# A softmax-attention backward kernel: part of every fourth K load moved to the first seven DMA engines

## The chip, the core and the metric

The kernel runs on one core of a Trainium2 chip. That core has a matrix engine (TensorE, "PE" in the profile, with its weight loads as "PEld"), a vector engine (DVE), a scalar engine (ACT), GpSimd (POOL) and SyncE (SP), which here only issues transfers, and it has 16 DMA engines that move data between the chip's memory (HBM) and the on-chip memory (SBUF). The metric is the device time of one execution in microseconds. Lower is better.

## The reference

One query row per head attends to 8192 keys; the forward output and the gradients of q, k and v are returned, all in bfloat16.

```python
B, H, Sq, Skv, Dh = 1, 32, 1, 8192, 128      # q, grad_out: (1,32,1,128)  k, v: (1,32,8192,128)

def _fwd_reference(q, k, v):
    scale = q.shape[-1] ** -0.5
    scores = jnp.einsum('bhqd,bhkd->bhqk', q, k) * scale
    attn = _softmax(scores, axis=-1)
    return jnp.einsum('bhqk,bhkd->bhqd', attn, v)

def reference(q, k, v, grad_out):
    _out, _vjp = jax.vjp(_f, q, k, v)         # _f is _fwd_reference
    _grads = _vjp(grad_out)
    return (_out, *_grads)                    # out, dq, dk, dv
```

For each head K and V (2 MB each) are read, and dk and dv (2 MB each) are written: 8 MB per head and 268 MB in all. dk and dv are outer products, so they are as large as K and V, and almost all of the traffic is in these four tensors.

## The kernel before

Each head's K is one tile of 128 partitions by 64 slots of 128 values: partition p holds the 64 consecutive rows 64p to 64p+63, which are 16 KB without a gap in HBM. A load of a whole K is one transfer of 128 rows of 16384 bytes. The pools hold three K tiles and two V tiles.

```python
CH = 16
K_BUFS = 3
V_BUFS = 2
NST = 2
# P = 128 partitions, NT = 64 slots, NCH = 4, H = 32 heads

    def rows_of(x, h, c, parts):
        L = NT // parts
        return x[0, h].rearrange("(p n) d -> p n d", p=P)[:, c * L:(c + 1) * L, :]

    def load_k(h):
        Kt[h] = kpool.tile([P, NT, D], BF16, tag="K", name="Kt")
        parts = NCH if h == 0 else 1
        for c in range(parts):
            nc.sync.dma_start(slots(Kt[h], c, parts), rows_of(k, h, c, parts))

    def load_v(h):
        Vt[h] = vpool.tile([P, NT, D], BF16, tag="V", name="Vt")
        parts = NCH if h in (0, H - 1) else 1
        for c in range(parts):
            nc.sync.dma_start(slots(Vt[h], c, parts), rows_of(v, h, c, parts))
    # ... (cut)
    def outer(h, which, r):
        # ... one quarter of dk or dv on DVE, then, for every half (a quarter in the last head):
        parts = 4 if h == H - 1 else NST
        if r % (4 // parts) == 4 // parts - 1:
            c = r // (4 // parts)
            nc.sync.dma_start(rows_of(dst, h, c, parts), slots(G, c, parts))
```

The main loop, cut to what issues transfers and what they serve; p_ is the head before:

```python
    for h in range(H + 1):
        p_ = h - 1
        if h < H:
            for u in range(NCH):
                k_blocks(h, u)              # DVE transposes K in blocks
            k_scores(h)                     # PE: scores
            if 0 < h < H - 1:
                load_v(h + 1)
        if h > 0:
            ds_of(p_); outer(p_, "dk", 0); dq_of(p_, 0)
        # ... (softmax of head h, partly)
        if h > 0:
            dq_of(p_, 1); outer(p_, "dk", 1)        # stores the first half of dk
        if 0 < h and h + 2 < H:
            load_k(h + 2)
        # ... (maximum, exp, sum)
        if h > 0:
            outer(p_, "dk", 2); outer(p_, "dk", 3)  # stores the second half of dk
        # ... (V transposes on PE, output, dP)
        outer(h, "dv", 0); outer(h, "dv", 1); outer(h, "dv", 2); outer(h, "dv", 3)  # two stores of dv
```

All these transfers are issued by SyncE on one queue. So a head has six of them: V, half of dk, K, half of dk, and two halves of dv.

Of the kernel before, what the change touches and what calls it, by code (L numbers as in the profile page):

```python
# [18 lines left out]
V_BUFS = 2  # L19
NST = 2  # L20
QD = 32


@with_exitstack
def kernel(
# [11 lines left out]
    nc = tc.nc  # L37
    P = 128
    _, H, S, D = k.shape
    assert D == P and S % (P * CH) == 0 and H <= P  # L40
    NT = S // P
    NCH = NT // CH
    NQ = P // QD
    assert NCH == 4 and NQ == 4
    W = D // 2
    NB = W // QD
    scale = float(D) ** -0.5
# [13 lines left out]
    Kt, Vt, XK, XV, st = {}, {}, {}, {}, {}  # L61
# [5 lines that stand above are left out]
    def slots(X, c, parts):  # L67
        L = NT // parts
        return X[:, c * L:(c + 1) * L, :]

    def load_k(h):
        Kt[h] = kpool.tile([P, NT, D], BF16, tag="K", name="Kt")
        parts = NCH if h == 0 else 1
        for c in range(parts):
            nc.sync.dma_start(slots(Kt[h], c, parts), rows_of(k, h, c, parts))

    def load_v(h):
        Vt[h] = vpool.tile([P, NT, D], BF16, tag="V", name="Vt")
        parts = NCH if h in (0, H - 1) else 1
        for c in range(parts):  # L80
            nc.sync.dma_start(slots(Vt[h], c, parts), rows_of(v, h, c, parts))

    rows = consts.tile([H, 2, D], BF16)
    nc.sync.dma_start(rows[:, 0, :], q.rearrange("b h s d -> (b h s) d"))
    nc.sync.dma_start(rows[:, 1, :], grad_out.rearrange("b h s d -> (b h s) d"))
    load_k(0)
    load_v(0)
    load_k(1)
    load_v(1)

    ident = consts.tile([P, P], BF16)
# [6 lines left out]
    nc.vector.reduce_sum(in_quad[:], ident[:].rearrange("p (a i) -> p a i", a=NQ), axis=AX.X)  # L98
    lane = consts.tile([P, QD], F32)
    nc.vector.reduce_sum(lane[:], ident[:].rearrange("p (a i) -> p i a", a=NQ), axis=AX.X)  # L100
# [3 lines left out]
    for w in range(NB):  # L104
        for e2 in range(2):
            four = consts.tile([H, NQ, QD], BF16, tag=f"four{w}{e2}")
            nc.vector.tensor_copy(
                four[:], rows[:, 0, :].rearrange("h (w j e) -> h w e j", w=NB, e=2)[:, w, e2:e2 + 1, :]
                .to_broadcast([H, NQ, QD]))
            tp = psT.tile([P, CH, P], BF16, tag="T")  # L110
# [17 lines left out]
    def k_blocks(h, u):  # L128


        if u == 0:
            XK[h] = ktpool.tile([P, CH, NB, NCH, QD], F32, tag="XK", name="XK_sb")
        nc.vector.transpose(XK[h][:, :, :, u, :],  # L133
# [94 lines left out]
# [3 lines that stand above are left out]
            x = st[h] = {}  # L231
            for u in range(NCH):
                k_blocks(h, u)
            k_scores(h)
            if 0 < h < H - 1:
                load_v(h + 1)
# [10 lines left out]
        if 0 < h and h + 2 < H:  # L247
            load_k(h + 2)
# [88 lines left out]
```

## Time and profile before

| | |
|---|---|
| time, median of three | 667.74 us (667.62 to 667.99) |
| span of the profiled execution | 667.0 us |
| PE busy | 516.8 us (77%) |
| DVE busy | 512.5 us (77%) |
| ACT busy | 182.1 us (27%) |
| bytes moved | 269.94 MB, mean 405 GB/s |
| HBM read, written | 134.23 MB each |

How to read it: the profile records each instruction of every engine and each packet of the DMA engines. "Busy" is the time in which an engine ran an instruction. The rows of 40 digits or numbers cut the span into 40 equal slices; a DMA digit of 9 means that in this slice the 16 DMA engines were busy for 90% or more on average. A DMA queue's share is the time its packets took on all 16 engines. A wait names who waited, at which line, for whom, and then the total in us, the number of waits and the longest. In the list of issues the last column is the median time from the issue of a transfer to its landing, which includes the time it stood behind earlier ones. [...]

### The profile page before, as it was taken

To read this page: it belongs to the slowest core of one execution; us is meant where nothing else is said; L and a number is where in the kernel's file an instruction comes from. 1 tells how busy PE (TensorE), PEld (TensorE's weight loads), DVE (VectorE), ACT (ScalarE), POOL (GpSimd) and SP (SyncE) were. 2 spreads that over 40 slices of the span, in tenths; PEclk is the share of its full clock that TensorE was granted. 3 is DMA by queue.
4 is the path that set the end of the run, shared out by engine and by line. 5 is a ranking of instruction groups with operands and counts; after the bars stand their busy time and mean duration, and the time that the engine had idled before them with its cause. 6 is when DMAs were issued, how large, how long until landed. Compare 5 with 4: busy or idle time off the path is not lost.

```text
span 667.0 us, 23105 instructions
## 1 busy us (share of the span) xinstructions
PE 516.8 (77%) x10727; PEld 485.8 (73%) x10727; DVE 512.5 (77%) x658; ACT 182.1 (27%) x321; POOL 0.7 (0%) x6
## 2 busy tenths in 40 slices
PE   2887988888887777878779787787776888778881
PEld 1887878878877767877668676677766777677870
DVE  4797888888877797777877778777788776887762
ACT  0333323232323222232222322223312223223230
POOL 0000000000000000000000000000000000000000
PEclk9995556566565565555555655666557665555555
DMA  8999999999999999999999999999999999999783
GB/s 330 414 425 424 419 427 414 424 423 426 425 425 424 425 425 424 425 429 423 423 427 426 423 416 422 413 412 418 395 423 418 397 416 406 409 420 403 270 357 142
DMA packets 29807, 269.94 MB, mean 405 GB/s; under 512 B 3472, under 2 KB 3472, under 8 KB 6032
## 3 DMA queue, kind: packets, MB, share of 16 engines
q1 hardware_dynamic: 29712, 268.48, 97.0%
q8 instruction: 83, 1.36, 0.7%
q14 instruction: 12, 0.10, 0.0%
HBM read 134.23 MB, written 134.23 MB: 403 GB/s over the span
## 4 chain that ended last, share of the span: by engine, by line
DMA 75%; PE 17%; DVE 3%; ACT 2%; issue 1%; SPq 0%; ACTq 0%
DMA Kt<-in_k_dram 26%; DMA Vt<-in_v_dram 26%; DMA out_dram<-G_dv 23%; PE T_ps L168 7%; PE s_ps L145 2%; PE dp_ps L185 2%; PE m_ps L185 2%; PE dp_ps L180 1%; DVE XK_sb L133 1%; ACT XT_sb L170 1%; PE m_ps L255 1%; DVE G_dk L195 1%; PE m_ps L268 1%; PE s_ps L161 0%; ACT qd L211 0%
## 5 line engine op out<-in xcount | busy, mean ns | idle before, releaser
L168 PE MATMUL T_ps<-ident,Vt 128*128 128x128 bf16 x2048 | 228.7, 302 | 31.9 <-DMA Vt<-in_v_dram 31.9
L168 PEld LDWEIGHTS <-Vt 128*128 128x128 bf16 x2048 | 201.1, 142 | 33.8 <-DMA Vt<-in_v_dram 33.6
L133 DVE STREAM_TRANSPOSE XK_sb<-Kt 128x1024 f32<-128x1024 f32 x128 | 148.2, 1213 | 81.1 <-DMA Kt<-in_k_dram 81.1
L170 ACT COPY XT_sb<-T_ps 128x1024 f32<-128x1024 f32 x128 | 129.5, 1012 | 189.7 <-PE T_ps L168 189.7
L195 DVE TENSOR_TENSOR G_dk<-ds_rep,qd 128x2048 bf16<-128x2048 bf16 x128 | 155.7, 1219 | 1.1
L195 DVE TENSOR_TENSOR G_dv<-p_rep,qd 128x2048 bf16<-128x2048 bf16 x128 | 148.2, 1220 | 8.5 <-ACT p_rep L277 8.5
L180 PEld LDWEIGHTS <-XT_sb 128*128 128x128 bf16 x2048 | 74.7, 106 | 27.2 <-ACT XT_sb L170 27.2
L180 PE MATMUL dp_ps<-doT,XT_sb 128*128 128x1 bf16 x2048 | 73.6, 166 | 24.4 <-ACT XT_sb L170 24.4
L145 PE MATMUL s_ps<-q_blk,XK_sb 128*128 128x4 bf16 x2048 | 59.1, 168 | 23.2 <-DVE pdt L216 20.5
L145 PEld LDWEIGHTS <-XK_sb 128*128 128x128 bf16 x2048 | 56.5, 103 | 25.5 <-DVE pdt L216 22.3
L185 PE MATMUL dp_ps<-ds_rep,Kt 128*128 128x1 bf16 x2048 | 64.7, 165 | 6.6 <-issue 6.0
L185 PEld LDWEIGHTS <-Kt 128*128 128x128 bf16 x2048 | 59.9, 104 | 12.3 <-issue 12.3
L185 PEld LDWEIGHTS <-Vt 128*128 128x128 bf16 x2048 | 61.1, 105 | 0.0
L185 PE MATMUL m_ps<-p_rep,Vt 128*128 128x1 bf16 x2048 | 60.5, 166 | 0.0
L226 ACT COPY dq_all<-dp_ps 128x1 f32<-128x1 f32 x32 | 5.1, 159 | 173.9 <-PE dp_ps L185 173.9
L268 PEld LDWEIGHTS m_ps<-rs,ones_f 128*128 128x128 f32 x64 | 16.0, 310 | 48.6 <-ACT e L267 48.6
L268 PE MATMUL m_ps<-rs,ones_f 128*128 128x1 f32 x64 | 18.7, 360 | 39.2 <-ACT e L267 39.2
L264 DVE TENSOR_REDUCE nbias<-m_ps 128x1 f32<-128x128 f32 x32 | 9.3, 292 | 22.0 <-ACT qd L211 22.0
L255 PE MATMUL m_ps<-diag,ones_f 128*128 128x128 f32 x64 | 25.3, 499 | 0.7 <-DVE diag L253 0.7
L218 DVE SCALAR_TENSOR_TENSOR ds_rep<-dp_ps,pdt,p_s 128x256 bf16<-128x256 f32 x32 | 15.5, 484 | 12.0 <-PE dp_ps L180 9.6
L277 ACT ACTIVATE p_rep<-e,rinv 128x256 bf16<-128x256 f32 x32 | 16.2, 507 | 30.3 <-DVE rinv L275 30.3
L211 ACT CAST qd<-m_ps 128x256 bf16<-128x256 f32 x32 | 11.9, 372 | 42.4 <-PE m_ps L207 42.4
(40 smaller groups left out, 163.0 us busy)
## 6 DMA issues: line engine op xcount, KB each, us to landing
Kt<-in_k_dram SPq DMA_DIRECT2D x31, 2048.0 KB, 28.0
out_dram<-G_dv SPq DMA_DIRECT2D x62, 1024.0 KB, 25.8
out_dram<-G_dk SPq DMA_DIRECT2D x62, 1024.0 KB, 28.0
Vt<-in_v_dram SPq DMA_DIRECT2D x30, 2048.0 KB, 28.3
Vt<-in_v_dram SPq DMA_DIRECT2D x8, 512.0 KB, 13.8
Kt<-in_k_dram SPq DMA_DIRECT2D x4, 512.0 KB, 5.4
out_dram<-G_dv SPq DMA_DIRECT2D x4, 512.0 KB, 16.9
out_dram<-G_dk SPq DMA_DIRECT2D x4, 512.0 KB, 10.7
```

Source lines behind the costliest of these rows:

```text
L133: nc.vector.transpose(XK[h][:, :, :, u, :], slots(Kt[h], u, NCH).rearrange("p g d -> p (g d)").bitcast(F32).rearrange("p (g w j) -> p g w ...
L145: nc.tensor.matmul(out[:, g, :], lhsT=cols[:, g, c // 2, c % 2], rhs=q_blk[:, h, c, :], start=(c == 0), stop=(c == 2 * NB - 1), skip_group ...
L168: nc.tensor.transpose(T_ps[:, i, :], Vt[h][:, c * CH + i, :], ident[:])
L170: nc.scalar.copy(X.rearrange("p c s -> p (c s)").bitcast(F32), T_ps.rearrange("p c s -> p (c s)").bitcast(F32))
L180: nc.tensor.matmul(st[h]["dp"][:, n:n + 1], lhsT=X[:, i, :], rhs=doT[:, h:h + 1], start=True, stop=True, skip_group_check=True)
L185: nc.tensor.matmul(out_col, lhsT=Xt[:, n, :], rhs=rep[:, n, 0:1], start=(n == 0), stop=(n == NT - 1), skip_group_check=True)
L195: nc.vector.tensor_tensor(slots(G, r, 4).rearrange("p n (a b) -> p n a b", b=R), slots(rep, r, 4).unsqueeze(2).to_broadcast([P, Q, D // R, ...
L211: nc.scalar.copy(x["qd"][:].rearrange("p a d -> p (a d)"), x["m"][:, 256:512])
L218: nc.vector.scalar_tensor_tensor(out=x["ds"][:], in0=x["dp"][:, 0:NT].unsqueeze(2).to_broadcast([P, NT, R]), scalar=pdt[:], in1=x["p_s"][: ...
L255: nc.tensor.matmul(x["m"][:, 128:256], lhsT=ones_f[:], rhs=diag[:], start=True, stop=True, skip_group_check=True)
L268: nc.tensor.matmul(x["m"][:, 0:1], lhsT=ones_f[:], rhs=rs[:], start=True, stop=True, skip_group_check=True)
L277: nc.scalar.activation(x["p"][:], e[:].unsqueeze(2).to_broadcast([P, NT, R]), ACT.Copy, scale=rinv[:])
```

## The change

Every fourth K load (heads 2, 6, 10, ..., 30) is no longer one transfer of 128 rows of 64 slots. It becomes three: all 128 partitions with slots 0 to 43, the first 119 partitions with slots 44 to 63, and the last 9 partitions with slots 44 to 63. The 119-row part is meant to run on the first seven DMA engines alone, so that these carry more of the traffic and the other nine less. Also, the V load of the last head is cut into halves instead of quarters. The bytes moved and all arithmetic are as before.

```diff
+LIGHT_EVERY = 4
+LIGHT_SLOTS = 20

     def load_k(h):
         Kt[h] = kpool.tile([P, NT, D], BF16, tag="K", name="Kt")
-        parts = NCH if h == 0 else 1
-        for c in range(parts):
-            nc.sync.dma_start(slots(Kt[h], c, parts), rows_of(k, h, c, parts))
+        if h == 0:
+            for c in range(NCH):
+                nc.sync.dma_start(slots(Kt[h], c, NCH), rows_of(k, h, c, NCH))
+        elif h % LIGHT_EVERY != LIGHT_EVERY // 2:
+            nc.sync.dma_start(Kt[h][:], rows_of(k, h, 0, 1))
+        else:
+            src = rows_of(k, h, 0, 1)
+            m = NT - LIGHT_SLOTS
+            for rng, cut in ((slice(0, P), slice(0, m)), (slice(0, 119), slice(m, NT)),
+                             (slice(119, P), slice(m, NT))):
+                nc.sync.dma_start(Kt[h][rng, cut, :], src[rng, cut, :])

     def load_v(h):
         Vt[h] = vpool.tile([P, NT, D], BF16, tag="V", name="Vt")
-        parts = NCH if h in (0, H - 1) else 1
+        parts = NCH if h == 0 else 2 if h == H - 1 else 1
```

## The prediction, made before the changed kernel was run

> **What bounds the kernel now.** I read the page from the DMA rows down: which resource is never idle, then who waits for whom, then how the 16 DMA engines differ. First the page's slices, queues and chain:
>
> ```profile
> DMA  8999999999999999999999999999999999999783
> GB/s 330 414 425 424 419 427 414 424 423 426 425 425 424 425 425 424 425 429 423 423 427 426 423 416 422 413 412 418 395 423 418 397 416 406 409 420 403 270 357 142
> q1 hardware_dynamic: 29712, 268.48, 97.0%
> q8 instruction: 83, 1.36, 0.7%
> ...
> DMA 75%; PE 17%; DVE 3%; ACT 2%; issue 1%; SPq 0%; ACTq 0%
> ```
>
> The queue keeps the 16 engines busy for 97% of the span, while PE and DVE stand at 77%; the chain is 75% DMA. So bytes per engine set the time, and the bytes are not changed. What can change is their share per engine. The stretches of the span show when a share is lost (columns: busy us of PE, PEld, DVE, ACT, POOL, then clock, DMA share, GB/s):
>
> ```profile
> 280.00:360.00 80.00, 64.70 (x1296) 60.92 (x1294) 61.02 (x77) 21.59 (x39) 0.00 (x0) 0.50 1.01 425
> ...
> 480.00:560.00 80.00, 60.52 (x1302) 56.57 (x1300) 63.27 (x80) 21.43 (x38) 0.00 (x0) 0.61 1.00 411
> ...
> 610.00:640.00 30.00, 24.28 (x510) 22.50 (x508) 24.26 (x34) 7.25 (x16) 0.00 (x0) 0.50 0.83 320
> 640.00:667.00 27.00, 11.00 (x236) 10.51 (x233) 9.37 (x14) 4.21 (x6) 0.00 (x0) 0.56 0.55 218
> ```
>
> 425 GB/s falls to 411 in the second half, and the last 57 us run at 320 and 218: some engines wait for others. The DMA queue's own waits say why:
>
> ```profile
> SPq L203 <- DMA out_dram<-G_dk: 111.7, 52, 2.5
> SPq L203 <- DMA Kt<-in_k_dram: 110.8, 26, 5.2
> SPq L75 <- DMA Vt<-in_v_dram: 97.5, 23, 4.5
> ```
>
> The issuing queue waits for earlier DMAs. In the trace the transfers use eight semaphores in turn, and from 400 to 610 us 60 of 61 issues come within 0.15 us of the last landing of the transfer eight places before; from 40 to 150 us only 1 of 36 does. So no engine can be more than eight transfers ahead of the slowest.
>
> Which engine is slow? The trace holds the 16 landing counts of every transfer. [...] For V loads issued at 83.15 and 383.48 us (15 heads apart) I get (us, landing):
>
> ```
> issued    first     8th    15th    last
>  83.15    97.8     99.1   101.9   101.9
> 383.48   391.2    399.7   402.1   411.8
> 590.66   598.2    600.6   606.5   619.0
> ```
>
> First engine: (391.15-97.79)/15 = 19.56 us per head. Last: (411.80-101.92)/15 = 20.66, and (618.98-411.80)/10 = 20.72 afterwards. ONE engine loses 1.1 us per head, is last in every transfer, and never rests until 666 us. Following the others, lags at 385 us are: seven engines at 0, 0.1, 0.2, 0.2, 0.3, 1.1 and 3.3; eight at 7.3 to 9.4; the slow one at 19.1. The eight are pushed back in turn by about 1.5 us at a time, with the instruction queue's fetches (q8, one packet of 0.9 to 1.1 us some 8 us apart). The slow one's store packets take up to 380 ns where the rest need 309; its load packets are as the others'.
>
> [...]
>
> I choose the reading that the slow one is engine 7, the seven fast ones are 0 to 6 and the eight that fetches hit are 8 to 15. The count 7 + 1 + 8 fits, and a split onto exactly the first seven fits it too. It is an inference.
>
> **The change, part by part.** Light heads are h = 2, 6, ..., 30: 8 loads of 31. Busy engines start a 16384 B packet every 0.607 us (611 ns less 4 overlap), an 8192 B one every 0.3055, a 4096 B one every 0.1553, by the packet records. The line through the outer two gives estimates of 0.419 us for 11264 B (44 slots) and 0.193 for 5120 B (20 slots); a completion packet takes 0.006.
>
> 1. K load before, per engine: 8*0.607+0.006 = 4.86 us.
> 2. Light load, engines 0-6: 8*0.419+0.006 + 17*0.193+0.006 + 0.193+0.006 = 6.84 us: +1.98.
> 3. Engines 7 and 8: 8*0.419+0.006+0.193+0.006 = 3.56 us: -1.31.
> 4. Engines 9-15: 3.36 us: -1.50.
> 5. Over 8 loads: engine 7 saves 10.5 us, and this all lies on the path, since that engine is busy from 3 to 666 us. Engines 0-6 gain 15.8 us of work, beside it.
> 6. Does another engine take over? Per head the slow one goes from 20.68 to 20.68-1.31/4 = 20.35. Engines 0-6: 19.56+1.98/4 = 20.06; the worst of them (its lag grew from 1.0 to 3.3 us in 15 heads, so 19.71) gets 20.21. Engines 8-15 lose 84/8 fetches of 1.5 us in 32 heads, 0.49 a head: 19.56+0.49-1.31/4 = 19.72 at most. It just holds.
> 7. Sixteen more issues: the queue issues some 0.5 us apart at the start (1.64, 2.10, 2.57), while transfers wait 5 to 25 us in the engines' rings. Hidden. But with eight semaphores in turn, a head of 8 transfers instead of 6 lets the queue reach one head ahead (8 MB, some 20 us) instead of 1.3. The slow engine still holds 15 us of work at each issue. Hidden.
> 8. Last V load in halves: four packets of 4096 B become two of 8192, 32*0.155-16*0.306 = 0.08 us less per engine, and two semaphores come free where the queue stalls near 626 us. Compute may start one quarter (1.3 us) later, but the tail has room: the last dk stores are issued at 651.4 to 655.8 and the slow engine reaches them only at 660.8.
>
> The tail: by the chain in order of time, compute goes from the landing of the last K (626.5) to the last store's data at 655.4. Both shift by the slow engine's gain, and the store backlog still ends later than compute. Sum: 667.74-10.5-0.1 = 657.1 us; a little for new collisions: 657.3, a gain of 1.6%.
>
> The issue table gives the sizes I used:
>
> ```profile
> Kt<-in_k_dram SPq DMA_DIRECT2D x31, 2048.0 KB, 28.0
> out_dram<-G_dv SPq DMA_DIRECT2D x62, 1024.0 KB, 25.8
> ...
> Vt<-in_v_dram SPq DMA_DIRECT2D x30, 2048.0 KB, 28.3
> Vt<-in_v_dram SPq DMA_DIRECT2D x8, 512.0 KB, 13.8
> ```
>
> **Rivals.**
> A. *The slow engine is among 9 to 15* (say 15) while 0 to 6 are free of fetches: it saves 8*1.50 = 12.0 us, 655.6. Against: eight engines are fetch-hit, and if those were the upper eight the slow one would lie in the lower eight.
> B. *The fetch-hit eight are engines 0 to 7.* Then 0-6 go to 19.56+0.49+0.50 = 20.55 per head against the old 20.68: a new bound takes the place of the old, at most 32*0.13 = 4 us are won, and the time stays at 663 to 667.
> C. *The slow engine is one of 0 to 6.* It gets 15.8 us more: 683.5. For: nothing in the trace numbers engines. Against: the seven fastest just fill that set.
> D. *Compute or the semaphores become the bound.* DVE waits 81.1 us for K in 24 waits and PE 31.9 us for V, so compute has slack of about 2.5 us a head (81.1/32) against a gain of 0.33; but the shorter reach of the queue in light heads could eat 1 to 4 us: 658 to 661.
>
> **Range and chances.** Main reading about 0.8, A 0.06, B 0.07, C 0.05. Within the main reading I expect 655.5 to 661. Faster by 2% means below 654.4, beyond even A; I give 0.08. Slower by 2% needs C (0.07). Range 654.6 to 663.
>
> **What would show it.** Right: the last landing runs behind the first by clearly less than 21 us from 400 us on (about 0.3 us growth per head instead of 1.1); K transfers of 1408, 595 and 45 KB; the slices stay near 425 GB/s to 600 us; the last-V landing moves from 639.7 to about 629; the final two slices hold higher rates. Wrong: seven engines last in each light load (B), or a lag that grows faster (C), or DMA share under 9 in the middle (D). The weakest link is the engine number.

## The result, and the profile after

The changed kernel takes 699.39 us (median of 4 runs, 698.27 to 700.65) against 667.68 us before: a ratio of 1.0477, 95% interval 1.0455 to 1.0499. That is 31.7 us slower, where 657.3 was predicted and 683.5 was the worst rival.

The slices, queue and chain of the changed kernel, in the form shown of before (40 equal slices of a span of 698.8 us):

```profile
DMA  8999999999999998999989999899998999979963
GB/s 334 396 424 424 425 425 357 421 424 427 402 329 422 424 425 356 339 425 423 425 349 344 427 425 422 339 359 426 428 424 315 379 426 426 426 286 389 418 277 137
...
q1 hardware_dynamic: 30576, 268.48, 94.2%
...
DMA 78%; PE 13%; DVE 5%; ACT 1%; issue 1%; SPq 0%; ACTq 0%; DVEq 0%
```

The same bytes now leave the 16 engines idle for 6% of the span instead of 3%. Between dips the rate is the old 425 GB/s; the dips recur at the pace of the light loads, one in four heads. The stretches of the span show it closely (columns as before: from:to, length, busy us of the five compute engines, clock, DMA share, GB/s). The first two are the stretches shown of before, the last two are one light load and the time after it:

```profile
280.00:360.00 80.00, 58.54 (x1200) 55.34 (x1199) 57.33 (x71) 21.67 (x36) 0.00 (x0) 0.55 0.97 393
480.00:560.00 80.00, 62.80 (x1325) 58.91 (x1323) 58.32 (x75) 22.04 (x39) 0.00 (x0) 0.59 0.96 391
...
270.00:295.00 25.00, 18.47 (x376) 17.33 (x373) 18.12 (x23) 6.67 (x11) 0.00 (x0) 0.50 0.90 332
300.00:345.00 45.00, 32.23 (x678) 29.68 (x675) 33.44 (x44) 11.91 (x23) 0.00 (x0) 0.58 1.01 426
```

393 and 391 GB/s stand against 425 and 411 before. The issue table of the changed kernel has the three parts as planned:

```profile
Kt<-in_k_dram SPq DMA_DIRECT2D x8, 1408.0 KB
Kt<-in_k_dram SPq DMA_DIRECT2D x8, 595.0 KB
...
Kt<-in_k_dram SPq DMA_DIRECT2D x8, 45.0 KB
```

The waits of the issuing queue, in the changed kernel, are still waits for earlier transfers:

```profile
SPq L215 <- DMA out_dram<-G_dk: 102.9, 50, 2.4
SPq L215 <- DMA Kt<-in_k_dram: 89.9, 20, 5.5
...
SPq L79 <- DMA Vt<-in_v_dram: 53.6, 12, 5.1
```

So DMA remains the bound, and the question is which engine is last. The completion counts of one light load answer it. In the trace of the kernel before, each of the 209 transfers, of 32 or 128 rows, has 16 of these counts on its semaphore, and there are as many packets of 4 B as counts, 3344. A count is read here as the landing of one engine's share, and its distance to the first count of the transfer as that engine's lag; no trace says which engine a count is from. The lags keep: from one 128-row transfer to the next, the counts put in order of time move against the first by 0.03 us in the median, and nine in ten by under 0.37. In the changed kernel the 128-row part has 16 counts, the 119-row part 7 and the 9-row part 9 (us; from the trace's semaphore times, without one further count that each of the two smaller parts has 0.4 to 0.7 us after its issue):

```
44 slots, 128 rows, issued 89.49:  102.4 102.5 103.2 103.9 104.0 104.0 104.1 105.3 105.9
                                   106.5 106.9 107.2 107.7 111.6 111.7 112.8
20 slots, 119 rows, issued 89.88:  111.8 112.0 112.9 113.7 117.3 117.7 118.7
20 slots,   9 rows, issued 92.35:  102.9 103.0 112.1 112.4 113.1 114.3 117.5 117.9 119.0
dk half,  128 rows, issued 94.85:  105.0 to 108.4 (nine), 114.4 to 121.2 (seven)
```

The part that was to go to fast engines ends at 118.7 and 119.0, and the last engine of the next transfer, 121.2, is one of the seven. This suggests that the slow engine is among those that were given more. Also, by the prediction's estimate the 119-row part should take 17*0.193 = 3.3 us per engine; matched in order, the seven take 5.2 to 6.0.

### The profile page after: what moved, and what is told of

Read it like the earlier page. It is cut to its first block, busy times and chain, and to the rows that moved or that the text cites. A ratio compares the mean times of both kernels' runs of the same rounds, so it can differ in the third digit from the quotient of the medians.

```text
span 698.8 us, 23136 instructions
## 1 busy us (share of the span) xinstructions
PE 521.1 (75%) x10727; PEld 489.5 (70%) x10727; DVE 513.9 (74%) x658; ACT 182.1 (26%) x321; POOL 0.7 (0%) x6
## 4 chain that ended last, share of the span: by engine, by line
DMA 78%; PE 13%; DVE 5%; ACT 1%; issue 1%; SPq 0%; ACTq 0%; DVEq 0%
DMA Kt<-in_k_dram 39%; DMA Vt<-in_v_dram 16%; DMA out_dram<-G_dv 15%; DMA out_dram<-G_dk 8%; PE T_ps L180 5%; DVE XK_sb L145 2%; PE s_ps L157 2%; PE m_ps L197 1%; PE dp_ps L197 1%; DVE G_dk L207 1%; PE dp_ps L192 1%; ACT XT_sb L182 1%; PE m_ps L267 1%; PE m_ps L280 0%; PE s_ps L173 0%
## 5 line engine op out<-in xcount | busy, mean ns | idle before, releaser
L180 PE MATMUL T_ps<-ident,Vt 128*128 128x128 bf16 x2048 | 231.9, 305 | 49.2 <-DMA Vt<-in_v_dram 49.0
L197 PEld LDWEIGHTS <-Kt 128*128 128x128 bf16 x2048 | 59.9, 104 | 11.7 <-issue 11.7
```

The costliest lines, as they stand in the source:

```text
L180: nc.tensor.transpose(T_ps[:, i, :], Vt[h][:, c * CH + i, :], ident[:])
L197: nc.tensor.matmul(out_col, lhsT=Xt[:, n, :], rhs=rep[:, n, 0:1], start=(n == 0), stop=(n == NT - 1), skip_group_check=True)
```

## The experiments

Theory 1: the slow engine is one of 0 to 6 (rival C), so the change gave it more bytes. Theory 2: the packets of parts that cover only some of the 128 partitions are themselves slow. Rivals: short packets, more transfers, or the row spacing in HBM. In every table of steps below, a step is the time from one transfer's last landing to the next one's last landing, all parts of a K taken as one. The engine landing last is taken to be engine 4 in all of these runs, except in the run with 12 slots on engines 0 to 3, which is not in the table. The engines were numbered in one run; the runs stood on several chips, so elsewhere the number 4 is an inference unless the run itself shows it.

**The last V in halves alone.**

```diff
-        parts = NCH if h in (0, H - 1) else 1
+        parts = NCH if h == 0 else 2 if h == H - 1 else 1
```

> The kernel before with the last V load in halves, K loads as before. Both theories put the loss into the light K loads, so the time stays at 667.7 within 1 us. If it is over 672, the tail is part of the loss.

Measured: 667.89 us against 667.97, ratio 1.0000 (0.9992 to 1.0009). This part of the change does nothing; the rest is in the K loads.

**Numbering the engines.** A tiny load of n rows has n counts, as the table below shows. Behind a V load, their lags tell the engines apart.

```diff
                 load_v(h + 1)
+                if 8 <= h < 24:
+                    n = h - 7
+                    nc.sync.dma_start(probe[0:n, n - 1, :], rows_of(v, h + 1, 0, 1)[0:n, 0, :])
```

> The kernel before with one tiny extra load (n rows of 256 B, never used) behind the V load of heads 9 to 24, n = 1 to 16, so that it runs on n engines. Its landings next to those of the V load ahead of it number the engines by their lag. Theory 1 (the slow engine is one of 0 to 6, my rival C): the largest lag, some 14 to 20 us, shows up in a tiny load with n of 7 or less, and in all later ones. My prediction (the slow one is engine 7): it shows up first at n = 8. Time 667 to 673 in both.

Measured: 668.38 us in one run, and these landings (us after the first landing of the V load ahead):

```
n=4   0.3 0.4 0.9 1.7                                  V: last 11.5
n=5   0.4 0.4 0.9 2.5 12.8                             V: last 12.6
n=6   0.3 0.4 0.9 2.5 7.7 13.8                         V: last 13.6
n=7   0.4 0.5 1.7 2.5 7.7 7.7 14.9                     V: last 14.7
n=8   0.2 0.4 0.5 1.6 2.5 7.7 9.2 16.8                 V: last 16.6
n=15  0.2 0.2 0.4 0.5 0.7 1.2  5.2 5.3 5.4 6.8 6.8 7.3 9.1 10.0  18.7
n=16  0.2 0.2 0.3 0.4 0.5 1.5 2.1  4.0 4.1 4.2 5.6 7.5 8.1 8.6 9.6  18.5
```

Each load's lags come again in the next one's, moved by at most 1.9 us from n=4 to n=8, beside one more. So the engines are numbered here in the order in which rows bring them in: engine n is the one that a load of n+1 rows adds. The largest lag, 12.8 us, appears with the fifth row: the slow engine is engine 4. The sixth and seventh add middle lags, the eighth a small one. Going on in this way to 16, the fast engines are 0, 1, 2, 3, 7, 8 and 15, and the eight with middle lags, which the prediction took to be hit by instruction fetches, are 5, 6 and 9 to 14. Transfers of 119, 9, 28, 124, 5 and 4 rows show 7, 9, 14, 4, 5 and 4 counts; that k counts come from engines 0 to k-1 is inferred from the nested lags of the tiny loads.

**Bytes added to engines 0 to 3, or 0 to 4.** Extra loads that nothing reads; the second run adds engine 4 and nothing else.

```diff
+    spare = consts.tile([P, 2, 46, D], BF16)
     def load_k(h): ...
+        if h % 2 == 1:
+            hs = min(h, H - 2)
+            nc.sync.dma_start(spare[0:17:4], k[0, hs:hs + 2].rearrange(
+                "a (p n) d -> p a n d", p=P)[0:17:4, :, 0:46])   # 0:13:4 for four rows
```

> The kernel before with 16 extra loads (every odd head) of 4 rows, each 2 pieces of 11776 B, never used, on engines 0 to 3 alone[...]: 16*2*0.438 = 14.0 us more work for each of the four. Theory 1 (engine 4 is the slow one and sets the end; engines 0 to 3 have over 18 us of room): 668 to 670. If any extra transfer or any lag costs: 675 to 683.

> The same with 5 rows, so that engine 4 gets the 14.0 us too. Theory 1: 667.9+14.0 = 682, within 2 us. My prediction's reading (engine 7 is the slow one): as with 4 rows, 668 to 670.

Measured: four rows 667.71 us against 667.89 (ratio 0.9998, 0.9990 to 1.0007); five rows 687.29 (1.0290, 1.0275 to 1.0306). Theory 1 is shown, and on another chip than the numbering: 14 us of work on four engines cost nothing, and the same on engine 4 besides costs 19.4. The size missed by 5.4: by the table below, the extra loads and the dk stores behind them take 15.3 us more, dv 3.0 and V 1.3. Why engine 4 loses more than its added work stays open.

The slices of the five-row run (GB/s) show the signature of a slower last engine, a low level without the dips:

```profile
GB/s 335 419 422 422 426 424 421 428 423 425 423 428 426 424 426 424 413 422 425 411 402 412 415 387 400 387 387 408 384 385 387 407 409 375 392 391 391 228 386 140
```

**The split without a shift of bytes.** Two parts, both on all partitions.

```diff
-            for rng, cut in ((slice(0, P), slice(0, m)), (slice(0, 119), slice(m, NT)),
-                             (slice(119, P), slice(m, NT))):
+            for rng, cut in ((slice(0, P), slice(0, m)), (slice(0, P), slice(m, NT))):
```

> Light K loads in two parts on all 128 partitions (44 and 20 slots), so no engine gets more bytes; last V in halves. If bytes on the slow engine and slow packets on seven engines are the cause: 668 within 1.5 us, packets of 5120 B at 196 to 200 ns. If short packets or the extra transfers cost by themselves: 5120 B packets near 270 ns and 672 to 680.

Measured: 669.26 us against 667.97 (1.0020, 1.0010 to 1.0030). Packets of 5120 B take 196 ns in the median and 200.8 on average. In the changed kernel they take 212 in the median and 273 on average. Short packets are not the cause.

**The split in pieces of 28 rows.** I meant these to run on seven engines, and the expectation says so. They ran on 14: the trace shows 14 counts for 28 rows, so two rows each. So this run moves almost no bytes: by these counts engines 0 to 13 have 9 rows of 20 slots instead of 8, an estimated 8*0.193 = 1.5 us in all.

```diff
+            for rng, cut in ((slice(0, P), slice(0, m)), (slice(0, 28), slice(m, NT)),
+                             (slice(28, 56), slice(m, NT)), (slice(56, 84), slice(m, NT)),
+                             (slice(84, 112), slice(m, NT)), (slice(112, P), slice(m, NT))):
```

> Light K loads with nearly the same bytes per engine as the change (17 rows of 20 slots on engines 0 to 6 instead of 18, one on the others), but cut into four parts of 28 rows (4 rows per engine) and one of 16. Estimate from bytes alone: 8*(1.98-0.19) = 14.3 us more than before, 682. Theory 2 (the 119-row part is slow, 273 ns a packet on average instead of 196[...]): with 4 rows per engine packets go back to 196 to 215 ns and the time to 681 to 685. Rival (any transfer on seven engines is slow): packets stay near 270 ns and the time near 697 to 701.

Measured: 684.73 us (1.0263, 1.0243 to 1.0283), 16.8 us more, and 5120 B packets at 291 ns on average. The time fell where the text expected it, but for another reason: it is not the bytes. Six parts to a K also mean that the queue, which waits for the transfer eight places back, reaches less far, so this run alone does not tell slow packets from a short reach. The next two do.

**The same bytes in halves of the partitions, and the control.** Three parts in both; in the first, two of them cover 64 partitions each, in the second all three cover all 128.

```diff
# halves of the partitions
+            for rng, cut in ((slice(0, P), slice(0, m)), (slice(0, 64), slice(m, NT)),
+                             (slice(64, P), slice(m, NT))):
# control
+            for rng, cut in ((slice(0, P), slice(0, m)), (slice(0, P), slice(m, m + 10)),
+                             (slice(0, P), slice(m + 10, NT))):
```

> Light K loads in three parts: 44 slots of all partitions, then 20 slots of partitions 0 to 63, then of 64 to 127. Each part is on all 16 engines and each engine gets as many bytes as before[...]. Theory 2[...]: 5120 B packets well over 250 ns on average, time 672 to 685. Rival (slow because only few engines move the part, or because of the bytes): 5120 B packets at 196 to 205 ns and 668.5 to 670.5, as the split on all partitions gave.

> Control for the run with partition halves: light K loads in three parts again (44, 10 and 10 slots), each on all 128 partitions[...]. Theory 2: 668.5 to 670.5, all packets at their usual pace (11264 B at 422 ns, 2560 B near 103). Rival (three transfers, or the shorter reach of eight semaphores, cost the 12 us): 677 to 682.

Measured: halves 679.62 us (1.0174, 1.0157 to 1.0191), control 672.50 (1.0066, 1.0051 to 1.0081). Packets of 5120 B in the halves take 286 ns on average; those of 2560 B in the control 106, with a median of 102. Each run was timed beside the kernel before (667.89 and 667.69 us), so the halves cost 11.7 us and the control 4.8. Theory 2 holds so far: with the same bytes and the same number of parts, parts of 64 partitions have slower packets and cost 11.7-4.8 = 6.9 us. Packets of 5120 B alone do not do it, by the run in two parts (200.8 ns on average). The control also missed its expectation by 2: three parts cost 4.8 us on their own. The rates (halves, then control) show both, dips from the first light load on, and dips in the second half only:

```profile
GB/s 339 378 421 426 425 421 381 423 421 427 413 410 424 423 427 405 383 426 427 421 378 374 429 425 422 364 378 427 424 423 361 382 425 428 423 342 384 425 313 141
```

```profile
GB/s 326 414 423 425 427 420 422 423 425 426 421 427 426 424 425 421 411 425 425 425 390 385 427 426 425 382 398 427 425 423 364 395 426 430 421 341 390 422 297 142
```

What the control's own 4.8 us are made of can be seen in one place of its trace, though nothing was run to find its cause. Near 518.1 us thirteen 16384 B packets of a V load start within 0.4 us and take 0.9 to 1.6 us instead of 0.61; from 521.8 to 524.2 most of that load's packets take 0.7 to 2.4 us again. Engine 4 is then in its 10-slot parts, and its 2560 B packets take up to 618 ns instead of 102. In the light loads from 330 us on, its step is 5.3 to 5.9 us, against 5.0 in the three before that. Such bunches are in the kernel before too, and more often in the stretch in which the queue waits for engine 4: 18 of 3501 packets of 16384 B take over 700 ns from 110 to 380 us, and 266 of 2875 from 380 to 610 us.

**The rows lying back to back in HBM.** The changed kernel with a dense source for the 119-row part; it loads other values of K in these places.

```diff
+                if rng.stop == 119:
+                    f = LIGHT_SLOTS * D
+                    x = k[0, h].rearrange("s d -> (s d)")[0:119 * f].rearrange(
+                        "(p n d) -> p n d", p=119, d=D)
```

> The changed kernel, but the 119-row part reads 119 rows of 5120 B that lie back to back in HBM, instead of 5120 B out of every 16384 (it loads other values of K than the reference uses in these places; bytes, partitions and engines are the same). Theory 2[...]: packets stay near 270 ns on average, 696 to 701. Rival (the spacing of the rows in HBM makes the packets slow): near 200 ns and 683 to 690.

Measured: 697.70 us (1.0444, 1.0429 to 1.0460), packets 269 ns on average. The spacing in HBM is worth about 1.7 us (699.39-697.70) of the 31.7.

**Larger store packets.** Engine 4's own weakness is on stores; does it lose per packet?

```diff
-NST = 2
+NST = 1
```

> The kernel before with dk and dv stored whole (rows of 16384 B) instead of in halves of 8192 B, except in the last head. Engine 4 loses its 1.0 us per head on store packets. If it loses a fixed time per packet, half the packets save some 0.5 us a head: 651 to 655. If it loses per byte: 666 to 669. If later stores starve the queue or hold the two buffers: over 672.

Measured: 672.81 us (1.0077, 1.0060 to 1.0094). The last engine's steps over all dk and dv stores sum to 345.4 us against 343.9 before, with half the packets. From 110 to 380 us a whole dk store takes 5.28 us on average and a whole dv store 5.61, against 2*2.63 and 2*2.78 for the halves before. So the loss goes with the bytes. The time is still 5.1 us longer, and the expectation's third branch, a starved queue, is not the reason. The issuing queue does wait for compute now instead of earlier transfers:

```profile
SPq L75 <- PE dp_ps L185: 163.7, 29, 7.6
SPq L203 <- DVE G_dv L195: 162.7, 33, 14.6
```

But after the first 10 us each transfer is issued at least 5.7 us before the last engine has finished the transfers ahead of it, so that engine does not run dry. The excess is in its K steps: 163.7 us in sum against 159.8, with five of nine steps at 5.5 to 6.0 us instead of 4.9 from 426 us on. What slows these loads was not tested.

**Aimed at engine 4.** Parts of 124 and 4 rows show four counts each, read as engines 0 to 3 alone. First 12 slots in every fourth K, then 20 slots in every twelfth.

```diff
-LIGHT_SLOTS = 20
+LIGHT_SLOTS = 12                # second run: LIGHT_EVERY = 12, LIGHT_SLOTS = 20
-            for rng, cut in ((slice(0, P), slice(0, m)), (slice(0, 119), slice(m, NT)),
-                             (slice(119, P), slice(m, NT))):
+            for rng, cut in ((slice(0, P), slice(0, m)), (slice(0, 124), slice(m, NT)),
+                             (slice(124, P), slice(m, NT))):
```

> The change aimed by theory 1: 12 slots of every fourth K load in parts of 124 and 4 rows, on engines 0 to 3 alone, so that engine 4 is relieved. By bytes alone engine 4 saves 8*(4.86-3.96) = 7.2 us and engines 0 to 3, which have some 37 us of room by their own pace, get 23 us: 660.5 to 662. If the slow packets of theory 2 hit here as well[...]: 668 to 690.

> The light load on engines 0 to 3 in a smaller dose: 20 slots of the K loads of heads 6, 18 and 30 only, in parts of 124 and 4 rows. Engine 4 saves 3*1.50 = 4.5 us; engines 0 to 3 get 3*4.7 = 14 us, and by what the 12-slot run lost some 2 us a light load more. Theory 1 with these engines' room (14 us cost nothing): 663 to 665. If the slow packets or the longer waits reach engine 4: 667 to 670.

Measured: 673.95 us (1.0095, 1.0076 to 1.0114) and 664.67 (0.9945, 0.9932 to 0.9959). In the first run the last engine's dv step is 2.43 us in the median, the pace of a fast engine, against 2.65 before, so the bound is no longer engine 4 but, by its pace and the bytes added, one of engines 0 to 3. Their 3072 B packets took 150 ns on average, with 121 for the fastest twentieth. The smaller dose saves 3.4 us of the 4.5 computed. Engine 4 is not last throughout: the first dose, near 90 us, makes a step of 7.9 us instead of 4.9, because its lag is still small there and engines 0 to 3 land last for some heads. The run is faster than both kernels, by 0.55% of the kernel before, and this is the most that any run here won with the change's idea. Its slices and issues:

```profile
GB/s 331 417 421 421 427 420 409 424 423 427 423 430 423 425 424 428 423 427 425 422 394 384 424 423 427 421 428 427 422 428 420 427 424 420 420 313 381 423 353 145
...
Kt<-in_k_dram SPq DMA_DIRECT2D x3, 1408.0 KB, 18.5
```

Three dips, one for each light load, stand at slices 7, 21 and 22, and 36, where the changed kernel has eight.

## Why the prediction was wrong

Steps of the last landing engine, summed over the run (us; changes against before in brackets):

```
                          K              V              dk             dv            sum
before                159.8          159.2          169.2          174.7
split, two parts      159.9 (+0.1)   160.1 (+0.9)   167.0 (-2.2)   176.5 (+1.8)      +0.6
control, three parts  162.9 (+3.1)   159.7 (+0.5)   167.5 (-1.7)   176.6 (+1.9)      +3.8
halves of partitions  167.9 (+8.1)   165.9 (+6.7)   165.9 (-3.3)   175.5 (+0.8)     +12.3
pieces of 28 rows     164.7 (+4.9)   172.5 (+13.3)  166.6 (-2.6)   175.5 (+0.8)     +16.4
five rows added       159.6 (-0.2)   160.5 (+1.3)   184.5 (+15.3)  177.7 (+3.0)     +19.4
dense source          189.0 (+29.2)  160.5 (+1.3)   165.7 (-3.5)   177.2 (+2.5)     +29.5
changed kernel        196.1 (+36.3)  160.9 (+1.7)   163.5 (-5.7)   174.2 (-0.5)     +31.8
```

The sums account for each run's span against the 667.0 of before (changed kernel 698.8, halves 679.5). In the five added rows' line, their own landings are counted within the dk step behind them.

- **What bounds the kernel: right.** One engine is never idle and sets the end; the pair with four and five added rows shows it. That it is last in every transfer holds only from about 100 us on: of the V load issued at 83.15 us the last two landings are 0.01 us apart.
- **"I choose the reading that the slow one is engine 7": this step failed.** It was read from a count (7 fast, 1 slow, 8 hit by fetches) and from the change's own choice of seven engines, while nothing in the trace of before numbers them. That the three parts go to 16, 7 and 9 engines, which steps 2 to 4 take for granted, is what the changed kernel's counts agree with. The count of seven, one and eight was right and the places were not: the slow engine is 4, and 5 and 6 have middle lags. So step 5's saving of 10.5 us went to engines 7 and 8, which had time to spare, and step 2's +1.98 us per light load fell on the engine that sets the end. Rival C had this, with a chance of 0.05 (0.07 stands a few lines later for the same case; the two do not agree), and its 683.5 us is bytes alone.
- **The estimate of 0.193 us per 5120 B packet (step 2) held only in a part that covers all 128 partitions.** On all 128 rows it was right (196 ns, less the overlap). In the 119-row part it was not. Engine 4's eight light loads sum to 74.6 us against 8*4.86 = 38.9. Of these 35.7, bytes account for 15.8 by step 2's estimate. The 128-row parts take 35.0 instead of 26.9, +8.1, all in the first four light loads, when the other engines of the seven are close ahead in their 119-row part. The 119- and 9-row parts take 39.6 instead of 27.9, +11.7. Afterwards 4.5 us come back, mostly in dk steps: 15.8+8.1+11.7-4.5 = 31.1 of 31.7.
- **Why such parts are slow was not shown.** By the counts an engine has 128/16 = 8 rows of a 128-row transfer and 119/7 = 17 of the 119-row part, so at least nine of the 17 lie on partitions that it does not write in a given 128-row transfer. The halves against their control show the loss without a shift of bytes (packets of 5120 B at 286 ns on average, where the split in two parts had 200.8; 6.9 us). But which engine writes which partition is in no trace.
- **Step 7, "hidden": half right.** The slow engine does hold work at each issue, as the step says: after the first 10 us, every transfer of the control is issued at least 7.6 us before the last engine has finished those ahead of it, and so in the changed kernel. So a short reach leaves no gap on that engine, which is how rival D's loss of 1 to 4 us could have come about. Yet with two parts the extra transfers cost 1.3 us, with three 4.8. The bunches of slow packets are what the control's trace shows beside it; whether the short reach makes them, and how much of this cost lies within the 31.7, was not separated.
- **Step 8 and the tail: right.** Halves of the last V change nothing to be seen (ratio 1.0000).

My own signs of being wrong showed up, but not sorted by rival. "Seven engines last in each light load", set down for B, is what the counts show, with rival C's engine among them; DMA digits of 8 in the middle, set down for D, are there too. C's sign, a lag that grows faster, is not: in V loads the last landing falls behind the first from 8.0 us (issued at 83 us) to 20.0 (340 us), against 4.1 to 18.6 before.

## What to carry to other kernels

A load balance over DMA engines needs the number of the slow engine, and here sixteen tiny transfers of 1 to 16 rows gave it in a single run; without that, the bytes moved here landed on the engine that sets the end (31.7 us slower). Before tuning shares, add work to the engines thought idle and to the one thought slow: the pair shows who has room. In these runs splitting K loads into parts that cover only some of the 128 partitions cost time of its own (6.9 us in the halves, against their control), so the dose should be small and the saving counted after that cost.

## What was not expected of the hardware

- Engine 4 is slow on this kernel's stores and loses with bytes, not with packets: from 110 to 380 us its steps in the kernel before are 2.63 us (dk) and 2.78 (dv) on average, where 8*0.3055+0.006 = 2.45 is the usual pace, about 1.0 us in a head of 20.7. Its load steps, 4.88 to 4.90, are near the usual 4.86. Why engine 4 differs was not found.
- Instruction fetches set eight of the engines back in turn, each time by about 1.5 us: in the kernel before, the lags of the 8th to the 15th landing grow by 55.6 us in sum from 100 to 381 us, with 37 fetches between (by the numbering these engines are 5, 6 and 9 to 14). Over the run, 83 fetches make that an estimated 83*1.5/8 = 15.6 us per engine.
- An estimated 14 us of extra work (16*2*0.438) on four engines cost nothing (667.71 us against 667.89), and on a fifth 19.4 (687.29): more than was added.
- Later in the run, when the faster engines have to wait for engine 4, load packets come in bunches that take up to 2.2 us (2.4 in the control) instead of 0.61, thirteen of them starting within 0.4 us in the place looked at. Whether the waiting makes them is open.
